# Routing attention and a PReLU feed-forward on one core: general-path test from the denominators, queries' clusters by DMA, members on ScalarE, fetch apart from split

## The chip, the cores and the metric

The kernel runs on one NeuronCore of a Trainium2 chip. The core has five engines with a queue of their own, each worked off in the order in which the program was written: TensorE (PE, matrix products; its weight loads are shown as PEld), VectorE (DVE), ScalarE (ACT), GpSimd (POOL) and SyncE (SP, which here only starts DMA transfers). They wait for each other by semaphores. SBUF is the working memory of 128 partitions, PSUM the eight banks that TensorE writes to. The metric is device time in microseconds (us) of one execution, as the median of several.

## The reference

Attention over 4 batches, 8 heads, 768 positions and a head size of 64, in which a query sees only the keys whose nearest of 16 centroids (by cosine) is its own, followed by a two-layer feed-forward with a PReLU:

```python
q_assign = np.argmax(np.einsum('bhsd,hcd->bhsc', q_n, c_n), axis=-1)
k_assign = np.argmax(np.einsum('bhsd,hcd->bhsc', k_n, c_n), axis=-1)
mask = q_assign[:, :, :, None] == k_assign[:, :, None, :]
scores = scale * np.matmul(q, k.transpose(0, 1, 3, 2))
scores = np.where(mask, scores, -1000000000.0)
attn = np.exp(scores - np.max(scores, axis=-1, keepdims=True))
attn = attn / (np.sum(attn, axis=-1, keepdims=True) + 1e-09)
attn_out = np.matmul(attn, v)
...
x = np.ascontiguousarray(attn_out.transpose(0, 2, 1, 3)).reshape(B * S, H * D)
h = x @ w_in
g = np.maximum(h, 0.0) + alpha * np.minimum(h, 0.0)
return g @ w_out
```

q, k, v and centroids are float32. The two weight matrices (512 x 2048 and 2048 x 512) and alpha arrive as the program's inputs; the weights are float64, and the kernel makes float32 of them itself out of their two 32-bit words.

## The kernel before, in words

**Pairs, units, steps.** Work goes by pairs n of two heads: n = 4 b + hp, 16 pairs. A unit is a pair and a half of its 384 queries, and it goes over the 6 chunks of 128 keys. The order of units is: batch, half, pair of heads, so four units make one block of 384 token rows over all 512 columns, and eight such blocks go to the feed-forward. A unit has three steps u, so there are 96 steps, NS. Steps 0 to 11 make the first block with attention alone; from step 12 on (UB) the feed-forward of the block before is woven in. Up to step 23 (TOGETHER is 24) a step treats two chunks; from step 24 on a unit treats its six chunks in two halves of three at its beginning, and the rest of its time is feed-forward, which the document calls the later stage.

**Slots.** A step has five slots: `tick()` at the beginning of each runs the pieces that `later(k, ...)` had put k slots ahead. In steps up to 23 the first two slots hold scores (`score`) and the weighing of what was scored the step before (`weigh`), the other three feed-forward pieces (`feed`) and preparations of later pairs (`prepare`). In the later stage a unit has three slots for its attention and twelve others, and a list `todo` of twelve entries is worked off, one in each, before the feed-forward piece of that slot: three masks, five additions into `acc`, the turn of `acc` with its row sums, an empty entry, `total`, `invert`. A block has 28 pieces: 16 `hidden` (four matrix products each and two evictions on ScalarE) and 12 `final` (four products each). `whole * left // 48` spreads them over the 48 slots of a block. After the last slot of a unit one more piece is fed where an accumulation is unfinished. When step 24 begins, two pieces have been kept back.

**Scores to output.** `score` multiplies keys by queries into a PSUM tile `sps` (two of them; the third chunk of a half uses two `fps` banks) and ScalarE takes Exp into one of the E tiles (L483, L486). For the pairs 0 to 3 (`n < NCH`) the cluster mask is a further product into the same bank (L475): `member` holds for each key a row of 0 or minus 2^60 per cluster, `aq` the queries' one-hot clusters. For later pairs VectorE masks (L499). `weigh` multiplies E by v into the single `vps` bank (L577), and for the first block also sums the denominators with a product by ones into `first_den` (L570). Otherwise denominators come from additions of E on VectorE (`add_up`, L510), a transposition and a row sum (`turn` L516, `rows_sums` L522, tile `part`), and a small product by `fold` (`total`, L532) into `mps`, the only bank of pool `ps_m`, which the products for similarities (`prep_sims`, L352) and clusters (`prep_clusters`, L397) use too. `invert` (L542 on) takes reciprocals and spreads them with two transpositions into `rd`; `normalise` (L606) multiplies `vps` by it into `xT`.

**Preparing a pair.** For pairs 0 to 3: `prep_features` transposes q and k on TensorE and ScalarE copies them out (L315, L319) in the step four ahead of the pair's first unit; three steps ahead of the pair's first unit `prep_sims` makes similarities, and one slot later `prep_argmax` finds each row's cluster on VectorE: transposition L360, maxima and comparisons L365 to L378, transposition to `member` (L382), and two scalings of its lower half by the columns of `pick` (L385). One step ahead of each of the pair's units `prep_queries` brings the queries' rows of `member` to the partitions 64 to 127 of `aq` (L425), two pieces of 32 rows. Later pairs return from `prep_argmax` before `member`; `prep_blocks` (VectorE), `prep_clusters`, `prep_keys` and transpositions (L429) take the place.

**Squares.** For every pair and each of q and k, `square` lets ScalarE square the raw tile four slots later, in place, with the sum of each row in `squares` (L327). At the end the greatest of these sums and the lowest denominator (`lowest`, L544, L587) make `good`; a product by ones makes a flag (L834) that decides whether a slow general path is run. With these inputs it is not.

**Weights.** 32 blocks of 128 x 512 numbers are converted one after the other in three stages: fetch and `split` (VectorE, L239, L241), four slots later `scale` (ScalarE, L245, L247), two slots later `join` (VectorE L251, L254; GpSimd L257). Five `raw` tiles are used in turn, so a fetch waits for the join of five conversions before. `converting` begins 15 of them in steps 0 to 11 and two in each step after that. `convert_up_to` would run a conversion at once if a feed-forward piece needed it.

**SyncE's queue** holds, in the program's order, the loads of q, k, v, the fetches of weights and the output rows.

Of the kernel before, what the change touches and what calls it, by code (L numbers as in the profile page):

```python
# [9 lines left out]
FP32 = mybir.dt.float32  # L10
BF16 = mybir.dt.bfloat16
U32 = mybir.dt.uint32
I32 = mybir.dt.int32
AF = mybir.ActivationFunctionType
ALU = mybir.AluOpType
AX = mybir.AxisListType
PS = bass.MemoryType.PSUM
P = 128
# [3 lines left out]
def kernel(  # L22
# [11 lines left out]
    nc = tc.nc  # L34
# [4 lines left out]
    NJ = S // P  # L39
# [4 lines left out]
    SCALE = float(D) ** -0.5  # L44
# [45 lines left out]
    def later(slots, piece):  # L90
        due.setdefault(now[0] + slots, []).append(piece)
# [8 lines left out]
    NP = len(pairs)  # L100
    raw_qk, vts = {}, {}

    Q = 32
# [127 lines left out]
    def convert(src, dst):  # L231
        raw = raw_tiles[0]
        raw_tiles.append(raw_tiles.pop(0))
        nc.sync.dma_start(out=raw.rearrange("p n w -> p (n w)"), in_=src)
        lo, hi = raw[:, :, 0], raw[:, :, 1]
        power = cvt.tile([P, CW], U32, name="power")

        def split():
            nc.vector.tensor_scalar(out=power, in0=hi, scalar1=0x7FF00000, scalar2=None,  # L239
                                    op0=ALU.bitwise_and)  # L240
            nc.vector.tensor_scalar(out=dst.bitcast(U32), in0=hi, scalar1=0x000FFFFF,  # L241
                                    scalar2=None, op0=ALU.bitwise_and)

        def scale():
            nc.scalar.activation(out=power, in_=power, func=AF.Relu,  # L245
                                 bias=low_exp[:, 0:1], scale=8.0)
            nc.scalar.activation(out=dst, in_=dst.bitcast(U32), func=AF.Identity,  # L247
                                 bias=1.0, scale=2.0 ** -20)

        def join():  # L250
            nc.vector.scalar_tensor_tensor(  # L251
                out=power, in0=hi, scalar=0x80000000, in1=power,
                op0=ALU.bitwise_and, op1=ALU.bitwise_or)
            nc.vector.scalar_tensor_tensor(  # L254
                out=dst, in0=lo, scalar=2.0 ** -52, in1=dst,
                op0=ALU.mult, op1=ALU.add)
            nc.gpsimd.tensor_tensor(out=dst, in0=dst, in1=power.bitcast(FP32),  # L257
                                    op=ALU.mult)
        return [split, scale, join]

# [34 lines left out]

    squares = const.tile([P, 2 * NP], FP32, name="squares")  # L300
    lowest = const.tile([P, 2 * NP], FP32, name="lowest")
    BOUND = 30.0 / SCALE


    qkTs, firsts, aqs = {}, {}, {}
# [3 lines left out]
    def prep_features(n, g):  # L309
        if n not in qkTs:  # L310
            qkTs[n] = qkp.tile([P, NB * P], FP32, name="qkT")
        ps = misc()
        for i, t in enumerate(groups[g]):
            w, j = divmod(t, NJ)
            nc.tensor.transpose(out=ps[:, i * P:(i + 1) * P],  # L315
                                in_=raw_qk[n, w][:, j].rearrange("p h d -> p (h d)"),
                                identity=ident)
        t0, m = groups[g][0], len(groups[g])
        later(1, lambda: nc.scalar.copy(qkTs[n][:, t0 * P:(t0 + m) * P],  # L319
                                        ps[:, 0:m * P]))  # L320
        for w in range(2):
            if t0 < (w + 1) * NJ <= t0 + m:
                square(n, w)

    def square(n, w):
        raw = raw_qk.pop((n, w)).rearrange("p j h d -> p (j h d)")
        later(4, lambda: nc.scalar.activation(  # L327
            out=raw, in_=raw, func=AF.Square,
            accum_out=squares[:, 2 * n + w:2 * n + w + 1]))

    def prep_blocks(n, w):
        if w == 0:
            qkTs[n] = qkp.tile([P, NB * P], FP32, name="qkT")
        nc.vector.transpose(out=qkTs[n][:, w * S:(w + 1) * S],
                            in_=raw_qk[n, w].rearrange("p j h d -> p (j h d)"))
        square(n, w)

# [18 lines left out]
    def prep_argmax(n, ps):  # L358
# [23 lines left out]
        nc.vector.transpose(out=member[:, 0, :], in_=top.rearrange("p t c -> p (t c)"))  # L382

        for h in (1, 0):
            nc.vector.tensor_scalar(  # L385
                out=member[HP:P, h, :], in0=member[HP:P, 0, :],
                scalar1=pick[HP:P, h:h + 1], scalar2=pick[HP:P, h + 2:h + 3],
                op0=ALU.mult, op1=ALU.add)
        members[n] = member

    def prep_clusters(n):
# [24 lines left out]
    def prep_queries(n, half, h):  # L416

        if h == 0:
            aqs[n, half] = aqp.tile([P, 2, HS], BF16, name="aq")
        if n < NCH:  # L420

            if h == 0:
                r = slice(half * Q, (half + 1) * Q)
                for g in range(NG // 2, NG):
                    nc.scalar.copy(aqs[n, half][g * Q:(g + 1) * Q, 0, :],  # L425
                                   members[n][r, 0, :])
            return
        own_half = everys[n].rearrange("p g i r h -> p g (i r) h")[:, half, :, h:h + 1]
        nc.vector.transpose(out=aqs[n, half][:, h, :],  # L429
                            in_=own_half.broadcast_to((P, NX, Q)))  # L430
# [105 lines left out]
    def invert(n, half):  # L536

        if (n, half) not in totals:
# [1 line left out]
        ps = totals.pop((n, half))  # L540
        inv = rdp.tile([P, 2 * NX], FP32, name="inv")
        nc.vector.reciprocal(out=inv, in_=ps[:, 0:2 * NX])  # L542
        i = 2 * n + half
        nc.vector.tensor_reduce(out=lowest[:, i:i + 1], in_=ps[:, 0:2 * NX], axis=AX.X,  # L544
                                op=ALU.min)
        rd = rdp.tile([P, HS], FP32, name="rd")
        for h in range(2):
            r = slice(h * D, (h + 1) * D)
# [5 lines left out]
    def weigh(m, denominators=False):  # L554
# [24 lines left out]
        if denominators and done:  # L579
# [3 lines left out]
            nc.vector.transpose(  # L583
                out=denT[:, 0:NX // 2, :].rearrange("p x i -> p (x i)"),
                in_=first_den[:, 0:HS // 2])
            i = 2 * n + half
            nc.vector.tensor_reduce(out=lowest[:, i:i + 1], in_=denT[:, 0:NX // 2, 0],  # L587
                                    axis=AX.X, op=ALU.min)
            inv = rdp.tile([P, 2 * NX], FP32, name="inv")
            for g in range(P // Q):  # L590
                h, x = divmod(g, 2)
# [131 lines left out]
    for u in range(-AHEAD, TOGETHER):  # L723
# [31 lines left out]
            feed_block(u)  # L755
            whole = len(ffn) - KEEP
        take = (max(len(ffn) - KEEP - whole * (UB - 1 - u % UB) // UB, 0) if ffn else 0)
        converting = 0 if u < 0 else 1 + (u % 4 == 3) if u < UB else 2
        for i in range(SLOTS - FIRST):
            tick()  # L760
            feed(take * (i + 1) // 3 - take * i // 3)
# [10 lines left out]
    for u in range(TOGETHER, NS + 1):  # L772
# [4 lines left out]
        if s == 0 or u == NS:  # L777
# [24 lines left out]
                todo.append(lambda c=c, E=E: add_up(E[c]))  # L802
            todo.append(lambda n=n, half=half: (turn(n, half), rows_sums(n, half)))
            todo.append(lambda: None)
            todo.append(lambda n=n, half=half: total(n, half))
            todo.append(lambda n=n, half=half: invert(n, half))
            slots = range(3, SLOTS)
        else:
            slots = range(SLOTS)
# [14 lines left out]
    while due:  # L824
        tick()
    good = const.tile([P, 2], FP32, name="good")
    nc.vector.tensor_reduce(out=good[:, 0:1], in_=squares, axis=AX.X, op=ALU.max)
    nc.vector.tensor_reduce(out=good[:, 1:2], in_=lowest, axis=AX.X, op=ALU.min)
    nc.vector.tensor_scalar(out=good[:, 0:1], in0=good[:, 0:1], scalar1=BOUND,
                            scalar2=None, op0=ALU.is_le)  # L830
    nc.vector.tensor_scalar(out=good[:, 1:2], in0=good[:, 1:2], scalar1=0.0,
                            scalar2=good[:, 0:1], op0=ALU.is_gt, op1=ALU.mult)
    flag = misc()
    nc.tensor.matmul(out=flag[0:1, 0:1], lhsT=good[:, 1:2], rhs=ones[:, 0:1],  # L834
                     start=True, stop=True)
# [160 lines left out]
```

## Time and profile before

| | |
|---|---|
| median of three runs | 1034.42 us (1032.88 to 1034.53) |
| profiled execution | 1034.78 us, its span 1032.9 us |
| TensorE busy | 1000.6 us, 97% |
| VectorE busy | 668.5 us, 65% |
| ScalarE busy | 353.9 us, 34% |
| GpSimd busy | 50.0 us, 5% |
| first scores / first feed-forward product | 17.27 us / 89.11 us after the span's start |

How to read it: a group or a timeline entry names the line of the kernel, the engine, the operation, and the tile written and the tiles read. An entry of the timeline begins with its start and its duration in us; "x8" are eight instructions in a row (a float32 matrix product counts as two); what stands in brackets is how long the engine stood idle before it, and whose work ended the wait. Where an instruction waited for more than one thing, the one that came last is named. The list of waits adds such idle times up: us in total, times, the longest. The span is divided into 40 slices of 25.8 us, with the busy share of each in tenths; PEclk is the clock granted to TensorE, in tenths of full speed. Ends of TensorE's products are modelled.

### The profile page before, as it was taken

To read this page: it belongs to the slowest core of one execution; us is meant where nothing else is said; L and a number is where in the kernel's file an instruction comes from. 1 tells how busy PE (TensorE), PEld (TensorE's weight loads), DVE (VectorE), ACT (ScalarE), POOL (GpSimd) and SP (SyncE) were. 2 spreads that over 40 slices of the span, in tenths; PEclk is the share of its full clock that TensorE was granted. 3 is DMA by queue.
4 is the path that set the end of the run, shared out by engine and by line. 5 is a ranking of instruction groups with operands and counts; after the bars stand their busy time and mean duration, and the time that the engine had idled before them with its cause. 6 is when DMAs were issued, how large, how long until landed. Compare 5 with 4: busy or idle time off the path is not lost.

```text
span 1032.9 us, 10431 instructions
## 1 busy us (share of the span) xinstructions
PE 1000.6 (97%) x3923; PEld 487.7 (47%) x3923; DVE 668.5 (65%) x1159; ACT 353.9 (34%) x692; POOL 50.0 (5%) x71
## 2 busy tenths in 40 slices
PE   7789999999999999999999999999999999999997
PEld 4334444454454544445454454545445454544453
DVE  4788798687475766778666666868756675662111
ACT  5756554434231323424132232414323141321220
POOL 1222322000000000000000000000000000000000
PEclk9989999999999999999999999999999999999999
DMA  9633654030000233040000230213000000000000
GB/s 194 184 112 104 149 132 87 16 77 0 1 1 20 41 47 46 1 87 5 1 0 11 52 47 10 36 36 56 1 1 1 31 0 1 1 11 20 1 0 34
DMA packets 120938, 42.74 MB, mean 41 GB/s; under 512 B 113696, under 2 KB 113712, under 8 KB 120880
## 3 DMA queue, kind: packets, MB, share of 16 engines
q1 hardware_dynamic: 120704, 41.95, 18.5%
q8 instruction: 33, 0.54, 0.2%
q14 instruction: 25, 0.20, 0.1%
q10 hardware_dynamic: 176, 0.04, 0.0%
HBM read 35.69 MB, written 6.29 MB: 41 GB/s over the span
## 4 chain that ended last, share of the span: by engine, by line
PE 87%; DVE 8%; ACT 3%; issue 1%; POOL 0%; DVEq 0%; POOLq 0%; ACTq 0%
PE fps L649 30%; PE fps L629 29%; PE vps L577 11%; PE sps L465 9%; PE fps L465 3%; DVE acc L510 2%; PE mps L352 1%; DVE acc L516 1%; PE sps L475 1%; PE mps L532 1%; DVE gT L621 1%; DVE part L522 1%; PE fps L570 1%; ACT gT L636 0%; DVE power L251 0%
## 5 line engine op out<-in xcount | busy, mean ns | idle before, releaser
L629 PE MATMUL fps<-xT,w_in_sb 128*128 128x384 f32 x1024 | 342.2, 491 | 0.0
L649 PE MATMUL fps<-w_out_sb,gT 128*128 128x512 f32 x768 | 337.1, 595 | 1.1 <-DVE gT L621 1.1
L629 PEld LDWEIGHTS fps<-xT,w_in_sb 128*128 128x128 f32 x1024 | 191.3, 190 | 141.9 <-ACT raw L483 4.9
L649 PEld LDWEIGHTS fps<-w_out_sb,gT 128*128 128x128 f32 x768 | 144.6, 190 | 176.2 <-issue 164.3
L621 DVE SCALAR_TENSOR_TENSOR gT<-neg,alpha_neg,gT 128x384 f32<-128x384 f32 x128 | 81.2, 637 | 125.9 <-ACT neg L637 124.4
L636 ACT ACTIVATE gT<-fps 128x384 f32<-128x384 f32 x128 | 62.7, 490 | 273.5 <-PE fps L629 273.5
L465 PE MATMUL sps<-qkT 64*128 64x384 f32 x576 | 113.1, 512 | 0.1
L499 DVE SCALAR_TENSOR_TENSOR raw<-aq,key,raw 128x384 f32<-128x384 bf16 x160 | 88.8, 614 | 37.7 <-ACT raw L486 26.2
L486 ACT ACTIVATE E<-sps 128x768 f32<-128x768 f32 x88 | 67.2, 814 | 65.5 <-PE sps L475 39.3
L499 DVE SCALAR_TENSOR_TENSOR E<-aq,key,E 128x384 f32<-128x384 bf16 x128 | 71.3, 613 | 17.9 <-ACT E L486 12.2
L577 PE MATMUL vps<-E,vt 128*64 128x384 f32 x448 | 82.9, 498 | 0.0
L465 PEld LDWEIGHTS sps<-qkT 64*128 64x128 f32 x576 | 53.1, 192 | 53.1 <-issue 22.1
L510 DVE TENSOR_TENSOR acc<-acc,E 128x768 f32<-128x768 f32 x64 | 61.2, 956 | 15.0 <-ACT E L486 13.2
L657 DVE TENSOR_TENSOR y<-y,fps 128x512 f32<-128x512 f32 x30 | 20.6, 686 | 69.1 <-PE fps L649 69.1
L637 ACT ACTIVATE neg<-fps 128x384 f32<-128x384 f32 x128 | 62.1, 485 | 0.0
L486 ACT ACTIVATE raw<-sps 128x768 f32<-128x768 f32 x56 | 42.9, 815 | 53.2 <-PE sps L465 53.2
L655 ACT COPY y<-fps 128x512 f32<-128x512 f32 x24 | 14.0, 585 | 133.3 <-PE fps L649 133.3
L577 PE MATMUL vps<-raw,vt 128*64 128x384 f32 x320 | 56.5, 491 | 0.0
L577 PEld LDWEIGHTS vps<-E,vt 128*64 128x64 f32 x448 | 29.4, 137 | 41.1 <-issue 41.1
L510 DVE TENSOR_TENSOR acc<-acc,raw 128x768 f32<-128x768 f32 x48 | 45.9, 956 | 1.1
L465 PE MATMUL fps<-qkT 64*128 64x384 f32 x192 | 41.5, 509 | 0.0
L483 ACT ACTIVATE raw<-fps 128x384 f32<-128x384 f32 x48 | 21.0, 495 | 48.1 <-PE fps L465 48.1
(101 smaller groups left out, 642.0 us busy)
## 6 DMA issues: line engine op xcount, KB each, us to landing
raw<-in_moe_w_in_dram SPq DMA_DIRECT2D x16, 512.0 KB, 4.0
raw<-in_moe_w_out_dram SPq DMA_DIRECT2D x16, 512.0 KB, 3.5
vt<-in_v_dram SPq DMA_DIRECT2D x16, 384.0 KB, 4.2
out_dram<-y SPq DMA_DIRECT2D x24, 256.0 KB, 2.1
qk<-in_q_dram SPq DMA_DIRECT2D x48, 96.0 KB, 4.0
qk<-in_k_dram SPq DMA_DIRECT2D x48, 96.0 KB, 3.5
qk<-in_q_dram SPq DMA_DIRECT2D x8, 192.0 KB, 4.1
qk<-in_k_dram SPq DMA_DIRECT2D x8, 192.0 KB, 4.3
```

The costliest lines, as they stand in the source:

```text
L465: nc.tensor.matmul(out=bank(ps, h), lhsT=qkT[r:r + D, S + c * P:S + (c + 1) * P], rhs=qkT[r:r + D, half * HS:(half + 1) * HS], start=True, ...
L483: nc.scalar.activation(out=E[:, h, :], in_=ps[h][:, 0:HS], func=AF.Exp, scale=SCALE)
L486: nc.scalar.activation(out=E, in_=ps[:, :, 0:HS], func=AF.Exp, scale=SCALE)
L499: nc.vector.scalar_tensor_tensor(out=E[:, h, :], in0=aqs[n, half][:, h, :], scalar=keys[n][:, NJ + c, h:h + 1], in1=E[:, h, :], op0=ALU.is ...
L510: nc.vector.tensor_tensor(out=acc, in0=acc if first is None else first[3], in1=E, op=ALU.add)
L577: nc.tensor.matmul(out=po[r:r + D, 0:HS], lhsT=vts[n][:, h, c, :], rhs=e[:, h, :], start=(c == 0), stop=(c == NJ - 1))
L621: nc.vector.scalar_tensor_tensor(out=gs[f], in0=neg, scalar=alpha_neg[:, f:f + 1], in1=gs[f], op0=ALU.mult, op1=ALU.add)
L629: nc.tensor.matmul(out=ps[:, 0:HS], lhsT=w_in_sb[:, c, f * P:(f + 1) * P], rhs=xT[:, c, :], start=(c == 0), stop=(c == NCH - 1))
L636: nc.scalar.activation(out=gs[f], in_=ps[:, 0:HS], func=AF.Relu)
L637: nc.scalar.activation(out=neg, in_=ps[:, 0:HS], func=AF.Relu, scale=-1.0)
L649: nc.tensor.matmul(out=ps[:, 0:DM], lhsT=gs[f][:, i * P:(i + 1) * P], rhs=w_out_sb[:, f, :], start=on and f == f0, stop=off and f == f0 + ...
L657: nc.vector.tensor_tensor(out=ys[i], in0=ys[i], in1=ps[:, 0:DM], op=ALU.add)
```

## The change

- `squares` and `square` are gone. The test for the general path uses the denominators alone: a second reduction keeps their highest value beside the lowest, both over the float32 words read as integers, and `good` compares them with the words of 2^-40 and 2^50.
- The scaling of the lower half of `member` (two per pair, pairs 0 to 3) is done by ScalarE instead of VectorE.
- The queries' rows go from `member` to `aq` by DMA on SyncE's queue instead of by ScalarE.
- A conversion of weights has four stages: fetch, two slots later split, four slots later scale, two slots later join. The first begins in step 1 instead of 0, and two are begun in every third step instead of every fourth; 15 are again begun by step 11.
- In the later stage `todo` has a second empty entry ahead of `total`, and no `invert`; `invert` is called in the next unit, behind the first half of its scores, by the call that stood there already and had found nothing to do.

```diff
@@ convert
-        nc.sync.dma_start(out=raw.rearrange("p n w -> p (n w)"), in_=src)
         lo, hi = raw[:, :, 0], raw[:, :, 1]
         power = cvt.tile([P, CW], U32, name="power")
+
+        def fetch():
+            nc.sync.dma_start(out=raw.rearrange("p n w -> p (n w)"), in_=src)
...
-        return [split, scale, join]
+        return [fetch, split, scale, join]
@@
-    squares = const.tile([P, 2 * NP], FP32, name="squares")
     lowest = const.tile([P, 2 * NP], FP32, name="lowest")
-    BOUND = 30.0 / SCALE
+    highest = const.tile([P, 2 * NP], FP32, name="highest")
+    WORDS = [float((127 + e) * 2 ** 23) for e in (-40, 50)]
+
+    def check(n, half, dens):
+        i = 2 * n + half
+        for to, op in ((lowest, ALU.min), (highest, ALU.max)):
+            nc.vector.tensor_reduce(out=to[:, i:i + 1], in_=dens.bitcast(I32), axis=AX.X,
+                                    op=op)
@@ prep_features, square, prep_blocks
-        for w in range(2):
-            if t0 < (w + 1) * NJ <= t0 + m:
-                square(n, w)
-
-    def square(n, w):
-        raw = raw_qk.pop((n, w)).rearrange("p j h d -> p (j h d)")
-        later(4, lambda: nc.scalar.activation(
-            out=raw, in_=raw, func=AF.Square,
-            accum_out=squares[:, 2 * n + w:2 * n + w + 1]))
...
-        square(n, w)
@@ prep_argmax
         for h in (1, 0):
-            nc.vector.tensor_scalar(
-                out=member[HP:P, h, :], in0=member[HP:P, 0, :],
-                scalar1=pick[HP:P, h:h + 1], scalar2=pick[HP:P, h + 2:h + 3],
-                op0=ALU.mult, op1=ALU.add)
+            nc.scalar.activation(
+                out=member[HP:P, h, :], in_=member[HP:P, 0, :], func=AF.Identity,
+                scale=pick[HP:P, h:h + 1], bias=pick[HP:P, h + 2:h + 3])
@@ prep_queries
                 for g in range(NG // 2, NG):
-                    nc.scalar.copy(aqs[n, half][g * Q:(g + 1) * Q, 0, :],
-                                   members[n][r, 0, :])
+                    nc.sync.dma_start(out=aqs[n, half][g * Q:(g + 1) * Q, 0, :],
+                                      in_=members[n][r, 0, :])
@@ invert
-        i = 2 * n + half
-        nc.vector.tensor_reduce(out=lowest[:, i:i + 1], in_=ps[:, 0:2 * NX], axis=AX.X,
-                                op=ALU.min)
+        check(n, half, ps[:, 0:2 * NX])
@@ weigh
-            i = 2 * n + half
-            nc.vector.tensor_reduce(out=lowest[:, i:i + 1], in_=denT[:, 0:NX // 2, 0],
-                                    axis=AX.X, op=ALU.min)
+            check(n, half, denT[:, 0:NX // 2, 0])
@@ steps up to 23
-        converting = 0 if u < 0 else 1 + (u % 4 == 3) if u < UB else 2
+        converting = 0 if u < 1 else 1 + (u % 3 == 2) if u < UB else 2
@@ later stage
             todo.append(lambda n=n, half=half: (turn(n, half), rows_sums(n, half)))
             todo.append(lambda: None)
+            todo.append(lambda: None)
             todo.append(lambda n=n, half=half: total(n, half))
-            todo.append(lambda n=n, half=half: invert(n, half))
@@ the end
-    nc.vector.tensor_reduce(out=good[:, 0:1], in_=squares, axis=AX.X, op=ALU.max)
+    nc.vector.tensor_reduce(out=good[:, 0:1], in_=highest, axis=AX.X, op=ALU.max)
     nc.vector.tensor_reduce(out=good[:, 1:2], in_=lowest, axis=AX.X, op=ALU.min)
-    nc.vector.tensor_scalar(out=good[:, 0:1], in0=good[:, 0:1], scalar1=BOUND,
+    nc.vector.tensor_scalar(out=good[:, 0:1], in0=good[:, 0:1], scalar1=WORDS[1],
                             scalar2=None, op0=ALU.is_le)
-    nc.vector.tensor_scalar(out=good[:, 1:2], in0=good[:, 1:2], scalar1=0.0,
-                            scalar2=good[:, 0:1], op0=ALU.is_gt, op1=ALU.mult)
+    nc.vector.tensor_scalar(out=good[:, 1:2], in0=good[:, 1:2], scalar1=WORDS[0],
+                            scalar2=good[:, 0:1], op0=ALU.is_ge, op1=ALU.mult)
```

## The prediction

> **What bounds the kernel now.** I read the page's engine shares and slices first. The columns are busy microseconds, share of the span and instruction count, or tenths in 40 slices of 25.8 us.
>
> ```profile
> PE 1000.6 (97%) x3923; PEld 487.7 (47%) x3923; DVE 668.5 (65%) x1159; ACT 353.9 (34%) x692; POOL 50.0 (5%) x71
> ...
> PE   7789999999999999999999999999999999999997
> ...
> PEclk9989999999999999999999999999999999999999
> ```
>
> TensorE is the bound: from about 90 us on it is busy nearly without a break, and only work taken from it, or its own idle time, can shorten the program there. Before 90 us it has holes. So the second view is the list of what TensorE waited for (total us, times, longest):
>
> ```profile
> PE fps L315 <- ACT qkT L319: 9.2, 4, 4.1
> PE mps L532 <- ACT every L401: 7.1, 10, 1.0
> PE sps L475 <- ACT aq L425: 2.9, 2, 2.7
> PE mps L532 <- DVE part L522: 2.0, 7, 0.3
> ```
>
> Two places matter. L532 is the little matmul of `total`: 17 waits, 9.1 us, all after 230 us. L315 and L475 are the start. Third, the timeline around one wait at L532:
>
> ```profile
> 418.14 0.25 PE L397 MATMUL mps<-first,spread 128*128 128x24 bf16 x4
> ...
> 419.10 0.25 ACT L401 CAST every<-mps 128x96 bf16<-128x96 f32 x1
> ...
> 419.40 0.40 PE L532 MATMUL mps<-part,fold 128*128 128x24 f32 x2 [1.01 <-ACT every L401]
> ...
> 419.64 2.83 PE L629 MATMUL fps<-xT,w_in_sb 128*128 128x384 f32 x8
> ...
> 422.40 1.56 PE L465 MATMUL sps<-qkT 64*128 64x384 f32 x8
> ```
>
> `prep_clusters` (L397) fills the only `mps` bank, ScalarE must copy it out, and `total` needs the bank: 1.0 us idle, with a feed-forward piece of 2.8 us waiting just behind. In the seven short cases it is the row sum `part` that ends late (0.2 to 0.3 us). Fourth, the timeline of the start, which shows how ScalarE's order of work makes TensorE's holes:
>
> ```profile
> 23.34 1.51 ACT L486 ACTIVATE E<-sps 128x768 f32<-128x768 f32 x2
> ...
> 24.51 0.58 DVE L382 STREAM_TRANSPOSE member<-top 128x384 bf16<-128x384 bf16 x1
> ...
> 25.13 0.80 DVE L385 TENSOR_SCALAR member<-member,pick 64x384 bf16<-64x384 bf16 x2
> ...
> 25.36 1.56 PE L465 MATMUL sps<-qkT 64*128 64x384 f32 x8
> ```
>
> ```profile
> 39.40 1.52 ACT L486 ACTIVATE E<-sps 128x768 f32<-128x768 f32 x2 [0.65 <-PE sps L475]
> ...
> 43.43 0.58 DVE L382 STREAM_TRANSPOSE member<-top 128x384 bf16<-128x384 bf16 x1
> ...
> 45.33 0.72 ACT L245 ACTIVATE power<-power,low_exp 128x512 uint32<-128x512 uint32 x1 [3.29 <-DVE power L239]
> ...
> 46.48 1.49 ACT L486 ACTIVATE E<-sps 128x768 f32<-128x768 f32 x2
> ...
> 49.13 1.03 ACT L425 COPY aq<-member 32x384 bf16<-32x384 bf16 x2
> ...
> 50.82 1.12 PE L315 MATMUL fps<-ident,qk 128*128 128x128 f32 x4 [4.11 <-ACT qkT L319]
> ```
>
> An Exp (L486) runs as soon as its scores exist, except where ScalarE stands at something older: at 45.33 it waited 3.29 us for a split (L239) that stood on VectorE behind the cluster search. TensorE paid with 4.11 us idle.
>
> **The change, part by part.** Each term is against the profiled execution: 1034.78 us (span 1032.9 and 1.88 around it), 0.36 above the median 1034.42.
>
> *Total one slot later.* In the later stage a unit has 12 slots (0 to 11) and a block's 28 pieces go to 48 slots: after slot i of unit k, floor(7(47-i)/12) - 7k are left, that is 22, 22, 21, 21 at slots 8 to 11. Slot 10 always feeds a piece, slots 9 and 11 none. `total` stood in slot 10 before that piece and now stands in slot 11, after it. The piece's 2.7 us (final pieces: 3.5) is more than any of the 17 waits (at most 1.0). The exception is the first block, 30 pieces because two were kept: its units 0 and 2 feed in slots 9 and 11, so the wait at 236.23 (1.0 us) stays. Term: 9.1 - 1.0 = -8.1 us. `invert` moves behind the next unit's scores; on VectorE nothing lies between the two places. At 422.63 its reciprocal ran after the scores had begun anyway, so it costs nothing; the cover is 1.6 us until the first Exp is out, and VectorE's other 35% idle.
>
> *No squares.* 32 activations of 0.862 and 32 accumulator reads of 0.218: 34.6 us less on ScalarE, which is 34% busy. TensorE has no wait for a square in its list; zero. They also held the raw tiles: SyncE's queue waited 6.5 us on them in two places, and the loads behind were early enough; zero.
>
> *Second reduction.* 32 of 0.12 (24 columns) to 0.16 us (6 columns), 4 us of VectorE in its idle third. Zero; at the start four of 0.16 at most.
>
> *Queries' clusters by DMA.* 16 copies of 0.508 leave ScalarE, 16 DMAs of 24 KB enter SyncE's queue. No row shows an on-chip copy. Nearest by size: 8 and 32 KB landed in 3.0 and 2.3 us; behind a load it would be a load's 3.5 to 4.3. I take 4.3, as the first follows load(2). Ready at 14.5 (end of L382), needed at 19.75 by L475: 5.2 us, it fits by 0.9; the others have eight or more. Ends: 0 and +2 for the first alone. Behind each waiting copy stand the weights' fetches: the first starts near 14.7 either way, and those after the copy for pair 1 start at 25.1 or later and are split near 31 to 33. What is gained: ScalarE's 1.03 us ahead of L319 and the 2.9 us waits of L475.
>
> *Member on ScalarE.* L385 (0.383 on VectorE) becomes an activation; nearest rows: 0.490 for 128x384 (L636) and 0.508 (L425), so 1.0 a pair. The price is not this but the wait: ScalarE now stands at L382 with the next Exps queued behind, and the next scores wait for the Exps' banks. Worked for each pair:
> - Pair 0: ScalarE waited for the same L382 before (4.2 us, at the copies). Zero.
> - Pair 1: L382 ends 25.09, members 26.1, first Exp 26.9 instead of near 24.2; the next scores start at 27.0, not 25.36: +1.6.
> - Pair 2: the similarity matmuls end at 37.38, normalise at 38.17, the chain L360 to L382 takes 3.95 (10.55 to 14.50): 42.1. Members 43.1, one scaling (0.72 + 0.63) 44.5, then the Exps that ran at 39.40; first out at 45.3, TensorE was ready at 41.5: gap 3.8. After the 4.11 gap the granted clock fell, and against the same rows at full clock L315 took 1.12 for 0.66, L465 2.93 for 1.56, L475 0.82 for 0.50, L570 1.51 for 0.86: +2.8. So +6.6.
> - Pair 3: the same, +6.6.
>
> [...]
>
> *What is returned at the start.* Splits now run well ahead of their scaling (four slots, no longer behind the argmax), so the hold at 45.33 goes, and the copies at 49.13 with it: 4.11 + 2.8 = 6.9. The gap at 71.67 (2.66 + 0.22, then L577 2.35 for 1.51 and L465 2.37 for 1.56, 1.65) goes with the copies: 4.5. The copies at 30.11 sat in a gap of 1.20; half returns, 0.6. Together 12.0. Net: 14.8 - 12.0 = +2.8. Ends: +14.8 if nothing returns, -12.0 if the new waits are all covered. I stay near the middle since both sides come from the same in-order queue.
>
> *Conversions.* Fetch to join is 8 slots instead of 6, the first starts a step later; by step 12 both have begun 15, both begin the last in step 20. The last weights are joined by the start of step 22 and used in step 23; a raw tile has five slots between being free and being split, as before. Zero. VectorE's 9.5 us of waiting for the first fetches goes; behind it stood work that waited for L352 anyway.
>
> Sum: -8.1 + 2.8 = -5.3, so 1029.5 for a profiled execution, 1029.1 for the median.
>
> **Rivals.**
> - *ScalarE's new wait decides (slower).* Place: the Exps behind members of pairs 1 to 3. For it: strict order at 45.33. Against: the old holds should go. It decides as soon as the start loses over 8.1; at its full price +14.8 the net is +6.7: 1041.1.
> - *The start gains too.* VectorE is freed early, the members come before the Exps are ready. For: VectorE spent 9.5 us on DMA waits. Against: L352's time sets the chain. -8.1 - 12.0: 1014.3.
> - *The wait of total only moves.* If the bank or the row sum is late even after the piece, the change doesn't do what it seems to: 1034.4 + 2.8 = 1037.2. Against: 2.7 us of cover for 1.0.
> - *The copies land late.* First scores +2, each later one covered: 1031.
>
> **How the numbers follow.** Forecast 0.52, first rival 0.18, second 0.16, third 0.09, fourth 0.05. The forecast's own range is 1023 to 1034. The wider one runs from most of the second rival's way (1017) to just short of the first's full price (1040). Faster by over 0.2% (2.1 us, about what this measurement can tell from nothing) takes the forecast, the second and most of the fourth: 0.71. Slower takes the first and most of the third: 0.23; 0.06 between.
>
> **What will show it.** Right: no TensorE wait at L532 but one of 1.0 us in the first shared block; no wait of L475 for `aq`; gaps of about 3.8 us at the second-next scores after the similarity matmuls of pairs 2 and 3, with Exps behind the member activations; first feed-forward matmul near 92 instead of 89.1. Wrong: gaps at L532 as before, or the first feed-forward matmul after 97.

## The result: no difference, because two stages lost what the third gained

The changed kernel took 1033.88 us (median of four runs, 1032.59 to 1035.93), the kernel before 1033.86 beside it: a ratio of 1.0003, with a 95% interval of 0.9982 to 1.0024. The forecast was 1029.1. The profiled execution took 1034.77 us with a span of 1032.8, against 1034.78 and 1032.9 before, so the two profiles can be set side by side without a correction. The page of the changed kernel, its shares and slices:

```profile
PE 998.5 (97%) x3923; PEld 490.1 (47%) x3923; DVE 673.8 (65%) x1183; ACT 325.0 (31%) x620; POOL 52.5 (5%) x71
...
PE   7789999899999999999999999999999999999997
...
PEclk8899999999999999999999999999999999999999
```

Little of the change can be read there but ScalarE's busy time, 28.9 us less. The sum hides three stages that moved in different ways. I cut both traces at four instructions of TensorE: the first feed-forward product, the first scores of step 24, and the product for the general-path flag (L834 before, L828 after):

| stage | before | after | difference | forecast |
|---|---|---|---|---|
| start, to the first feed-forward product | 89.1 us | 92.8 us | +3.7 | +2.8 |
| middle, to step 24 | 119.5 | 128.5 | +9.0 | 0 |
| later stage, to the flag | 735.9 | 722.8 | -13.1 | -8.1 |
| end | 88.4 | 88.6 | +0.2 | 0 |

The list of TensorE's waits in the changed kernel answers the one shown of before (engine, line, whom it waited for: us in total, times, longest):

```profile
PE sps L463 <- ACT E L484: 10.3, 3, 4.0
PE fps L324 <- ACT qkT L328: 4.4, 3, 3.9
...
PE mps L351 <- DVE highest L310: 4.1, 2, 3.0
PE fps L623 <- DVE xT L600: 2.1, 1, 2.1
...
PE mps L530 <- DVE part L520: 1.3, 2, 0.7
...
PE mps L530 <- ACT every L399: 1.0, 1, 1.0
```

L530 is `total`, L532 before. Of its 17 waits of the later stage one is left, the 1.0 us in the first shared block; the two for `part` are new and lie in the middle (153 and 188 us). The waits of L475 for `aq` are gone, and three for Exps have come. L351 (`prep_sims`) and L623 (`hidden`) wait for VectorE, both in the middle. All line numbers from here on are those of the kernel that is spoken of.

The later stage, in the timeline of the changed kernel around the `total` that before stood at 419.40 with 1.01 us of waiting:

```profile
429.15 0.25 PE L395 MATMUL mps<-first,spread 128*128 128x24 bf16 x4
...
429.25 2.83 PE L623 MATMUL fps<-xT,w_in_sb 128*128 128x384 f32 x8
...
430.10 0.25 ACT L399 CAST every<-mps 128x96 bf16<-128x96 f32 x1
...
431.91 0.30 PE L530 MATMUL mps<-part,fold 128*128 128x24 f32 x2
...
432.14 1.56 PE L463 MATMUL sps<-qkT 64*128 64x384 f32 x8
```

The piece of 2.8 us lies where the gap was, ScalarE's copy is out 1.6 us before it is needed, and the scores follow `total` at once.

The start, in the timeline of the changed kernel:

```profile
45.85 0.58 DVE L381 STREAM_TRANSPOSE member<-top 128x384 bf16<-128x384 bf16 x1
...
46.47 1.43 ACT L384 ACTIVATE member<-member,pick 64x384 bf16<-64x384 bf16 x2 [5.03 <-DVE member L381]
...
47.92 0.72 ACT L247 ACTIVATE power<-power,low_exp 128x512 uint32<-128x512 uint32 x1
...
49.06 1.49 ACT L484 ACTIVATE E<-sps 128x768 f32<-128x768 f32 x2
49.91 2.93 PE L463 MATMUL sps<-qkT 64*128 64x384 f32 x8 [4.03 <-ACT E L484]
```

ScalarE stands idle for 5 us at the members, then does one scaling that had been due meanwhile, then the Exps; TensorE loses 4.03 us and runs the next scores in 2.93 instead of 1.56 us.

The middle, where the forecast had nothing, around the second wait of L351:

```profile
191.84 0.70 DVE L253 SCALAR_TENSOR_TENSOR power<-raw,power 128x512 uint32<-128x512 uint32 x1
...
192.44 0.70 DVE L256 SCALAR_TENSOR_TENSOR w_out_sb<-raw,w_out_sb 128x512 f32<-128x512 uint32 x1
193.05 0.70 DVE L253 SCALAR_TENSOR_TENSOR power<-raw,power 128x512 uint32<-128x512 uint32 x1
...
193.65 0.70 DVE L256 SCALAR_TENSOR_TENSOR w_out_sb<-raw,w_out_sb 128x512 f32<-128x512 uint32 x1
194.25 0.32 DVE L540 RECIPROCAL inv<-mps 128x24 f32<-128x24 f32 x1
194.47 0.14 DVE L310 TENSOR_REDUCE lowest<-mps 128x1 f32<-128x24 int32 x1
194.50 0.18 DVE L310 TENSOR_REDUCE highest<-mps 128x1 f32<-128x24 int32 x1
...
194.75 0.85 PE L351 MATMUL mps<-qkT,cT 128*32 128x384 f32 x8 [2.99 <-DVE highest L310]
```

The joins of two conversions (L253, L256) stand on VectorE directly ahead of the inversion, and the similarity products wait for the bank that the inversion reads. The same place before, where the wait was 0.44 us:

```profile
179.38 0.65 DVE L251 SCALAR_TENSOR_TENSOR power<-raw,power 128x512 uint32<-128x512 uint32 x1
...
179.95 0.68 DVE L254 SCALAR_TENSOR_TENSOR w_out_sb<-raw,w_out_sb 128x512 f32<-128x512 uint32 x1
...
181.60 0.30 DVE L542 RECIPROCAL inv<-mps 128x24 f32<-128x24 f32 x1
...
181.99 0.85 PE L352 MATMUL mps<-qkT,cT 128*32 128x384 f32 x8 [0.44 <-DVE lowest L544]
```

One join there, and the conversions' other stages are already done while TensorE is at its 7.1 us of output products. In the middle TensorE's waits grew from 1.5 to 8.3 us, and all of them are for VectorE. The gap of 2.07 us before L623 at 97.09 was followed by slow products: the granted clock was 0.58 from 97 to 100 us. The same 18 products, first in the changed kernel and then in "inversion first", an experiment below:

```profile
97.09 7.74 PE L623 MATMUL fps<-xT,w_in_sb 128*128 128x384 f32 x18 [2.07 <-DVE xT L600]
```

```profile
97.99 6.04 PE L623 MATMUL fps<-xT,w_in_sb 128*128 128x384 f32 x18 [1.94 <-DVE xT L600]
```

That is 1.7 us more. With the 6.8 us of waits it makes 8.5 of the 9.0.

### The profile page after: what moved, and what is told of

It is laid out like the page before. It is cut to its first block, busy times and chain, and to the rows that moved or that the text cites. A ratio compares the mean times of both kernels' runs of the same rounds, so it can differ in the third digit from the quotient of the medians.

```text
span 1032.8 us, 10335 instructions
## 1 busy us (share of the span) xinstructions
PE 998.5 (97%) x3923; PEld 490.1 (47%) x3923; DVE 673.8 (65%) x1183; ACT 325.0 (31%) x620; POOL 52.5 (5%) x71
## 4 chain that ended last, share of the span: by engine, by line
PE 87%; DVE 8%; ACT 2%; issue 1%; POOL 1%; DVEq 0%; POOLq 0%
PE fps L623 31%; PE fps L643 30%; PE vps L573 11%; PE sps L463 9%; PE fps L463 3%; PE mps L351 1%; DVE power L253 1%; DVE acc L508 1%; PE sps L473 1%; DVE w_out_sb L243 1%; ACT member L384 1%; DVE w_in_sb L256 1%; DVE power L241 0%; PE fps L324 0%; DVE w_out_sb L256 0%
## 5 line engine op out<-in xcount | busy, mean ns | idle before, releaser
L623 PE MATMUL fps<-xT,w_in_sb 128*128 128x384 f32 x1024 | 342.6, 492 | 2.1 <-DVE xT L600 2.1
L623 PEld LDWEIGHTS fps<-xT,w_in_sb 128*128 128x128 f32 x1024 | 192.1, 191 | 146.7 <-issue 7.8
L615 DVE SCALAR_TENSOR_TENSOR gT<-neg,alpha_neg,gT 128x384 f32<-128x384 f32 x128 | 78.3, 613 | 132.7 <-ACT neg L631 131.3
L463 PE MATMUL sps<-qkT 64*128 64x384 f32 x576 | 115.2, 520 | 10.3 <-ACT E L484 10.3
L497 DVE SCALAR_TENSOR_TENSOR E<-aq,key,E 128x384 f32<-128x384 bf16 x128 | 71.3, 613 | 11.9 <-ACT E L484 6.2
L508 DVE TENSOR_TENSOR acc<-acc,E 128x768 f32<-128x768 f32 x64 | 66.4, 1038 | 8.3 <-ACT E L484 6.5
```

Of the source, the lines that this page charges most:

```text
L463: nc.tensor.matmul(out=bank(ps, h), lhsT=qkT[r:r + D, S + c * P:S + (c + 1) * P], rhs=qkT[r:r + D, half * HS:(half + 1) * HS], start=True, ...
L497: nc.vector.scalar_tensor_tensor(out=E[:, h, :], in0=aqs[n, half][:, h, :], scalar=keys[n][:, NJ + c, h:h + 1], in1=E[:, h, :], op0=ALU.is ...
L508: nc.vector.tensor_tensor(out=acc, in0=acc if first is None else first[3], in1=E, op=ALU.add)
L615: nc.vector.scalar_tensor_tensor(out=gs[f], in0=neg, scalar=alpha_neg[:, f:f + 1], in1=gs[f], op0=ALU.mult, op1=ALU.add)
L623: nc.tensor.matmul(out=ps[:, 0:HS], lhsT=w_in_sb[:, c, f * P:(f + 1) * P], rhs=xT[:, c, :], start=(c == 0), stop=(c == NCH - 1))
```

## The experiments

Theory A: the middle's 9 us come from the conversions, whose stages stand later in the order of work on the engines. Rivals: they come from the start, whose delay is carried on (B); or a fetch apart from its split costs by itself. The table has all runs, with the stages from each profile (us), the median and the ratio to the kernel before on the same chip.

| kernel | start | middle | later | median | ratio, 95% interval |
|---|---|---|---|---|---|
| before | 89.1 | 119.5 | 735.9 | 1034 | |
| after | 92.8 | 128.5 | 722.8 | 1033.88 | 1.0003 (0.9982 to 1.0024) |
| after, old conversions | 94.0 | 119.7 | 722.8 | 1027.66 | 0.9940 (0.9924 to 0.9957) |
| after, members on VectorE | 91.0 | 128.6 | 722.8 | 1031.40 | 0.9969 (0.9956 to 0.9981) |
| before, later total alone | 87.6 | 119.5 | 722.8 | 1020.83 | 0.9873 (0.9857 to 0.9889) |
| after, neither | 87.7 | 119.7 | 722.8 | 1021.87 | 0.9883 (0.9866 to 0.9899) |
| after, five slots to the split | 101.5 | 129.3 | 722.8 | 1042.70 | 1.0075 (1.0057 to 1.0093) |
| before, new conversions alone | 91.8 | 128.7 | 735.9 | 1046.29 | 1.0107 (1.0088 to 1.0126) |
| after, neither, copies on ScalarE | 89.1 | 119.6 | 722.8 | 1022.06 | 0.9880 (0.9863 to 0.9898) |
| after, inversion first | 93.8 | 125.3 | 722.8 | 1031.38 | 0.9969 (0.9956 to 0.9982) |
| after, fetch two ahead | 94.0 | 119.7 | 722.8 | 1027.41 | 0.9942 (0.9924 to 0.9960) |
| after, fetch and split late | 90.2 | 128.6 | 722.8 | 1033.32 | 0.9998 (0.9989 to 1.0008) |
| the best parts | 83.0 | 120.6 | 722.8 | 1016.67 | 0.9843 (0.9818 to 0.9869) |

Middle and later stage repeat to 0.2 us between kernels of the same order; the start does not: "before" and "later total alone" run the same instructions there in the same order and took 89.1 and 87.6. So a difference of 1.5 us at the start means nothing. "After" and "fetch and split late" differ there by more than 2.5 us, with the same order on TensorE, VectorE, ScalarE and GpSimd.

**Old conversions.**

```diff
-        return [fetch, split, scale, join]
+        return [split, scale, join]
-        converting = 0 if u < 1 else 1 + (u % 3 == 2) if u < UB else 2
+        converting = 0 if u < 0 else 1 + (u % 4 == 3) if u < UB else 2
```

> The changed kernel with the conversions as before (fetch and split together, first in step 0). Between the first feed-forward product and step 24 the changed kernel took 128.5 us, the one before 119.5. Theory A: a conversion of four stages puts splits and joins into the first two slots of a step, on VectorE ahead of the inversion that the similarity products and the next normalisation wait for; that is the 9.0 us. It expects this stretch at 119 to 121 us, the start near the changed kernel's 92.8 (91 to 95), the later stage at its 722.8, and in all about 1025 us (1023 to 1028). Theory B: the stretch is long because the members on ScalarE make VectorE enter it late; then it stays at 126 us or more, and the whole at 1031 or more.

Middle 119.7 us, start 94.0, whole 1027.66. TensorE's waits in the middle of this kernel are those of before again:

```profile
PE fps L641 <- DVE gT L613: 1.1, 2, 0.9
...
PE mps L349 <- DVE highest L308: 0.5, 1, 0.5
```

The start is as long as in the changed kernel, and the middle is short all the same: rival B falls.

**Members on VectorE.**

```diff
-            nc.scalar.activation(
-                out=member[HP:P, h, :], in_=member[HP:P, 0, :], func=AF.Identity,
-                scale=pick[HP:P, h:h + 1], bias=pick[HP:P, h + 2:h + 3])
+            nc.vector.tensor_scalar(
+                out=member[HP:P, h, :], in0=member[HP:P, 0, :],
+                scalar1=pick[HP:P, h:h + 1], scalar2=pick[HP:P, h + 2:h + 3],
+                op0=ALU.mult, op1=ALU.add)
```

> The changed kernel with the members' scaling back on VectorE. The waits of TensorE for Exps behind the members (2.2, 4.0 and 4.0 us, and some 2.8 us of slow clock after each of the two long ones) should go: the first feed-forward product at 79 to 84 us instead of 92.8. Theory A: the stretch up to step 24 stays near 128 (126 to 131), in all about 1024 (1020 to 1028). Theory B: the stretch falls to about 120 as well, in all about 1013 to 1016.

The middle stayed at 128.6, as A says. The start did not fall to 79 to 84: the waits for Exps behind members are gone (0.6 us left), but others took their place. The first products for scores ran at 13.0 instead of 17.7 us, and their mask then waited 4.9 us for the first copy by DMA; further on TensorE lost 2.8 and 1.1 us to VectorE and 3.5 us to ScalarE's copies of features. My expectation had counted a wait as gone time without asking what is late next.

**Later total alone**, in the kernel before:

```diff
             todo.append(lambda: None)
+            todo.append(lambda: None)
             todo.append(lambda n=n, half=half: total(n, half))
-            todo.append(lambda n=n, half=half: invert(n, half))
```

> The kernel before with the later total and without the early inversion alone. From the profiles of the two kernels, units with a wait at the total lost 0.6 to 1.3 us in the changed kernel: step 24 to the flag 722.8 instead of 735.9. If that is this part's work: start 89.1 and middle 119.5 as before, later stage 722 to 724, in all 1020.5 to 1022.5. If instead the later stage gained from the squares' absence, the whole stays above 1027.

1020.83 us, with the later stage at 722.8 to the tenth. The whole gain of the change is in these two lines; the squares have no part in it. Which of the two it is, the later `total` or the inversion taken from behind it, no run separates.

**Neither** conversions nor members:

> The changed kernel with both undone: old conversions, members on VectorE; what is left of the change is no squares, the copies by DMA, the second reduction and the later total. If the two undone parts are all that was lost, the start is at most the 89.1 of before, less what the missing copies and squares gave TensorE (the 1.2 us gap, the 2.9 us waits): 82 to 89; the middle 119 to 121, the later stage 722 to 724, in all 1014 to 1022. If the copies by DMA cost something too, the start is above 89 and the whole above 1022.

1021.87 us, start 87.7. Its first scores wait in the same place as above. The timeline of this kernel:

```profile
13.92 0.58 DVE L379 STREAM_TRANSPOSE member<-top 128x384 bf16<-128x384 bf16 x1
...
14.67 2.32 SPq L422 DMA_DIRECT2D aq<-member  x2
...
19.35 0.98 PE L472 MATMUL sps<-aq,member 32*128 32x384 bf16 x4 [4.87 <-DMA aq<-member]
```

Issued at 14.67, there at 19.3. But the start as a whole is no longer than before, so others that went pay for this wait: the 4.11 us of before at 50.82 are 2.99 here, and the 1.20 at 31.80 and the 2.66 at 71.67 are gone, while 1.1 and 2.7 us of waiting for VectorE are new. From "neither", the new conversions add 9.5 us (to "members on VectorE"), the members on ScalarE 5.8 (to "old conversions"), and both 12.0: they overlap in part.

**Five slots to the split.** A first attempt to keep the fetch apart and move the stages out of the first two slots of a step:

```diff
-            later(4 if len(stages) == 2 else 2, lambda: stages and advance(stages))
+            later({3: 5, 2: 3, 1: 2}[len(stages)], lambda: stages and advance(stages))
```

> The changed kernel with five slots from fetch to split, then three to the scaling and two to the join: ten slots in flight instead of eight, but splits and joins now fall in the slots 2 to 4 of a step, where feed-forward pieces are fed, and none in its first two. Theory A (the place of the stages costs the middle its 9 us) expects the stretch from the first feed-forward product to step 24 at 119 to 122 us instead of 128.5, and in all 1024 to 1028. Rival (a fetch apart costs by the time in flight, by raw tiles coming free later): the stretch stays at 128 or grows, and the whole is 1034 or more.

Theory A, in the form that the first two slots of a step are the wrong place, falls here: no split and no join stands in them (the scalings on ScalarE do), and the middle is 129.3. The waits are partly others:

```profile
PE fps L643 <- DVE gT L615: 3.7, 2, 2.9
...
PE mps L351 <- DVE highest L310: 2.5, 1, 2.5
...
PE fps L623 <- DVE xT L600: 1.0, 1, 1.0
```

The slopes of the feed-forward now stand behind joins. The start grew to 101.5 with two gaps of 7.7 us before scores whose Exps stood late on ScalarE. The rival was right in its numbers; but this kernel changes both the time in flight and the order on the engines, so it could not say which.

**New conversions alone**, in the kernel before (the edit of the old conversions, turned round):

> The kernel before with the four-stage conversions alone. Theory A: the middle grows from 119.5 to 127 to 130 us with nothing else of the change there, the start stays at 87 to 93, the later stage at 735.9: 1041 to 1046 in all. If the middle's loss needs the other parts (members or copies elsewhere, the second reduction), it is below 1038.

1046.29 us: start +2.7, middle +9.2, later stage as before. The conversions need nothing else of the change to cost 12 us. This run also tests what the prediction expected of them at the start, that splits run ahead of their scaling and the 4.11 us gap at 50.82 goes:

```profile
44.12 0.72 ACT L247 ACTIVATE power<-power,low_exp 128x512 uint32<-128x512 uint32 x1 [2.72 <-DVE power L241]
...
46.79 1.03 ACT L427 COPY aq<-member 32x384 bf16<-32x384 bf16 x2
...
51.30 1.12 PE L317 MATMUL fps<-ident,qk 128*128 128x128 f32 x4 [4.46 <-ACT qkT L321]
52.34 2.93 PE L467 MATMUL sps<-qkT 64*128 64x384 f32 x8
```

ScalarE still waits 2.72 us for the split, the copies still stand behind it, and TensorE still loses 4.46 us and runs the next scores in 2.93 us instead of 1.56.

**Copies on ScalarE**, with conversions and members as before too:

> What is left of the change when conversions, members and the queries' copies are all as before: the later total, no squares, the second reduction. In the kernel with the copies by DMA the first scores waited 4.9 us for the first copy (issued at 14.67, landed at 19.3); by ScalarE it would be there at about 15.6. If that wait is on the path, the start is 84 to 86 us instead of 87.7 and the whole 1018 to 1020; if the start is set by VectorE anyway, it is 87 to 89 and the whole 1020 to 1023, as with the later total alone.

1022.06 us, start 89.1: as "neither" and as "later total alone", within their intervals. Taken together, the copies by DMA, the second reduction and the missing squares are worth nothing that these runs can tell, in either direction.

**Inversion first**, in the changed kernel:

```diff
+        if ended:
+            invert(*prior[:2])
         tick()
         if u >= 0:
             score(n, half, range(s, NJ, SB))
         tick()
-        if ended:
-            invert(*prior[:2])
```

> The changed kernel, with the inversion in steps up to 23 called ahead of the first slot of the next step instead of after its second: on VectorE it now stands before the split and the joins that fall into those two slots. Theory A expects the waits of the similarity products for the denominators' reductions (1.1 and 3.0 us) to go and the middle to fall from 128.5 to 122 to 126 us, the whole to 1027 to 1031; the wait of the first feed-forward products (2.1 us) and those at the total (0.6 and 0.7) stay. If the order ahead of the inversion is not the cause, the middle stays at 128 or more.

The waits of L351 fell from 4.1 to 0.6 us and the middle to 125.3; the whole, 1031.38, is just above what was expected. So the joins ahead of the inversion are the cause of L351's waits. The 3.2 us that the middle lost are not all theirs: the waits for `part` grew to 1.6, and one of 1.5 came at a `hidden` product, for an output addition on VectorE, so TensorE's waits fell by 1.8 us in all, from 8.3 to 6.5. The rest is mostly the 18 products at 97.99: they took 6.04 us here instead of 7.74, which is the pace of before (24 of them in 8.01 us from 89.11), although the gap before them, which the edit leaves alone, was still 1.94 us.

**Fetch two ahead.** The pair that separates the fetch from the order. Here each fetch is issued two conversions ahead of its split, while VectorE, ScalarE and TensorE have the order of "old conversions", instruction by instruction:

```diff
     def convert_next():
-        if sources:
-            under_way.append(convert(*sources.popleft()))
-            advance(under_way[-1])
+        if not fetched:
+            fetch_next()
+        if fetched:
+            under_way.append(fetched.popleft())
+            advance(under_way[-1])
+        while sources and len(fetched) < 2:
+            fetch_next()
...
-        converting = 0 if u < 1 else 1 + (u % 3 == 2) if u < UB else 2
+        converting = 0 if u < 0 else 1 + (u % 4 == 3) if u < UB else 2
...
+        if u == -1:
+            fetch_next()
+            fetch_next()
```

> The changed kernel with a fetch apart from its split, but another way: each fetch is issued two conversions ahead, and split, scaling and join stand in the slots they had before the change. On VectorE, ScalarE and TensorE the instructions are in the same order as in the kernel with the old conversions (middle 119.7, whole 1027.7); only SyncE's fetches stand earlier. Theory A, in the form that is left (it is where split, scaling and join stand on VectorE and ScalarE, two slots later): the middle is 119 to 121 us, the whole 1024 to 1029. Rival (a fetch apart from its split costs, for whatever reason): the middle is 126 or more, the whole 1034 or more.

Middle 119.7, whole 1027.41: the same as "old conversions" in every stage.

**Fetch and split late.** The reverse, with the order of the changed kernel on the three engines:

```diff
         def fetch():
-            nc.sync.dma_start(out=raw.rearrange("p n w -> p (n w)"), in_=src)
+            pass

         def split():
+            nc.sync.dma_start(out=raw.rearrange("p n w -> p (n w)"), in_=src)
```

> The reverse: the changed kernel, in which each fetch is issued only where its split stands, two slots late, so that fetch and split are together again; the order on VectorE, ScalarE and TensorE is that of the changed kernel. Theory A: the middle stays at 127 to 130 us and the whole at 1033 to 1038. Rival: the middle returns to 119 to 122 and the whole to 1024 to 1029.

Middle 128.6, whole 1033.32. The fetch's place has no effect, and the order of split, scaling and join has all of it. What VectorE itself waits for in the middle differs between the two orders. Before, and then after:

```profile
DVE power L239 <- POOL w_in_sb L257: 3.9, 3, 1.4
...
DVE power L239 <- POOL w_out_sb L257: 2.3, 2, 1.2
```

```profile
DVE power L241 <- POOL w_in_sb L259: 5.5, 4, 1.4
DVE power L241 <- POOL w_out_sb L259: 5.5, 4, 1.4
```

17 splits and 19 joins are begun in the middle in both. In the changed kernel eight splits wait 1.4 us each, all of them directly behind a join; before, five waited 1.2 to 1.4 us. Each starts 0.03 us after the end of the GpSimd product of the conversion three before it, and the pool that `power` comes from, `cvt`, has three buffers (`bufs=3`): what the split waits for is its buffer. That is 4.8 us more of waiting on VectorE, in order, ahead of all that stands behind. Besides, VectorE's busy time in the middle grew from 95.7 to 100.7 us. No run gave `power` a fourth buffer or took this waiting away by itself, so how much of the middle is due to it stays open.

**The best parts**: the later total, no squares, members on VectorE, the copies by DMA except the two for the very first scores, fetches two ahead.

```diff
+                    if (n, half) == (0, 0):
+                        nc.scalar.copy(aqs[n, half][g * Q:(g + 1) * Q, 0, :],
+                                       members[n][r, 0, :])
+                        continue
                     nc.sync.dma_start(out=aqs[n, half][g * Q:(g + 1) * Q, 0, :],
                                       in_=members[n][r, 0, :])
```

> A version from the parts that cost nothing: the later total, no squares, members' scaling on VectorE, the conversions' stages where they were with fetches two ahead, the copies by DMA except those for the very first scores, which ScalarE makes (their DMA kept TensorE waiting 4.9 us). If these waits of the start are on the path: start 82 to 86 us instead of 87.6 to 89.1, middle 119 to 121, later stage 722.8, in all 1015 to 1020. If the start is set by VectorE's own work: 87 to 89 and 1020 to 1023, no better than the later total alone.

1016.67 us, 0.9843 of the kernel before (0.9818 to 0.9869), and the shortest median of all kernels here. The start is 83.0. The waits for members, for the first copy and for `aq` are gone; the two longest of those that stay at the start are:

```profile
PE fps L337 <- ACT qkT L341: 7.2, 3, 3.9
...
PE vps L591 <- DVE xT L618: 2.7, 1, 2.7
```

So the parts of the change seem to help at the start where none of them opens a wait of its own: 83.0 is 4.6 us below "later total alone". The evidence is not strong. The intervals of these two kernels overlap, one of the four runs here took 1020.39 us, and "neither" differs in two things, the first copies and the fetches, which no run separates.

## Why the prediction was wrong

- *Conversions.* This is the step that failed: "Fetch to join is 8 slots instead of 6 ... a raw tile has five slots between being free and being split, as before. Zero." All that it checks holds: no weight came late, and a fetch's place is worth nothing (fetch two ahead). It asked when the weights are needed and when `raw` is free, and not which work stands behind the moved stages, nor when a buffer of `power` is free. On VectorE that work is the row sums, the inversion and the first block's last normalisation; the cost was +9.0 us in the middle, and 11.9 for the conversions alone. VectorE's idle third, which the prediction counts on for the second reduction and the inversion, is an average over the program; in the middle VectorE was busy for 95.7 of 119.5 us already before.
- *Total one slot later.* The mechanism was right to the piece: 16 of 17 waits went, the one in the first shared block stayed. The term was mis-sized: -8.1 was the idle time alone, and the stage gave -13.1. A unit with a wait of 1.01 us (28.92 us long) became 1.27 shorter, one with 0.31 became 0.67. The rest beside the idle time is 0.26 to 0.36 us in all but one of the 16 units that lost a wait (0.17 there), and up to 0.09 in units that had none. L532's weight load waited too (1.10 us idle at 419.40), and its two small products took 0.40 us together there, against 0.30 at the same place in the changed kernel (431.91), where nothing waited. That is 0.10 us of it; what the rest is was not shown.
- *Member on ScalarE.* Right: gaps of 2.2, 4.0 and 4.0 us for the 1.6, 3.8 and 3.8 worked out, with the scores after the long ones at 2.93 us as in the row that I had used. The activation took 0.70 us, not 0.5. That the gap of pair 1 would be followed by slow rows too (2.82 us for the scores instead of 1.56, at a granted clock of 0.54) I had not counted.
- *What is returned at the start.* The gaps at 31.80, 50.82 and 71.67 are gone and the start came out at +3.7 for +2.8, within what it varies by, but for the largest of these terms this was luck. The prediction gave 6.9 us to splits that run ahead. They do not: with the new conversions alone the gap stayed, at 4.46 us, and "old conversions" lacks it as the changed kernel does. In both, TensorE now idles in front of the scores instead (4.88 and 4.03 us). The copies by DMA shorten the gap: 2.99 us in "neither", 3.52 with the new conversions added. Of VectorE's 9.5 us of waiting for the first fetches, 5.0 stayed.
- *Queries' clusters by DMA.* Right in size: 4.6 us for the 4.3 taken. In the changed kernel ScalarE's members hid it, as the first scores come only at 17.7 us there; it showed where they were moved back.
- *No squares, second reduction.* Zero, as said.
- *The clock.* The granted clock was 0.54 in the 3 us after a gap of 2.2 us, 0.58 in the 3 us after one of 2.07, and 1.00 after one of 2.99. In these rows of the changed kernel a stretch and its length are followed by the busy time and instructions of PE, PEld, DVE, ACT and POOL, then by the granted clock; the last two columns are the DMA's share and GB/s:

```profile
29.00:32.00 3.00, 2.94 (x10) 1.20 (x12) 0.00 (x0) 0.71 (x2) 0.00 (x0) 0.54 0.81 277
97.00:100.00 3.00, 2.91 (x5) 1.63 (x6) 1.55 (x3) 1.65 (x4) 0.00 (x0) 0.58 0.00 0
194.75:197.75 3.00, 3.00 (x13) 1.21 (x14) 2.88 (x5) 0.00 (x0) 1.97 (x2) 1.00 0.01 1
```

The gap at 97.09 cost 1.7 us beside its own 2.07 (7.74 against 6.04 us for the 18 products). For each of the two gaps of 4 us the prediction had taken 2.8 us of slow rows, those behind the 4.11 us gap of before. That was too much: the scores took 2.93 us behind both, as there, but the mask's products 0.65 and 0.50 us for the 0.82 taken, the products by ones 0.86 for 1.51, and no products for features, 0.46 of the 2.8, stood behind these gaps. The slow rows cost 1.5 and 1.4 us.

Of the rivals none happened. The result lies inside the range of the forecast's own case, 1023 to 1034, for a reason that was in none.

## What to carry to other kernels

When a stage of work is moved by some slots, read on every engine what stands directly behind its new place and who waits for that; that its own result is still in time says nothing about it. Look at every buffer that the moved work uses, not only at the largest. An engine's idle share of the whole program is no cover in a stage in which it is fuller. That a sum of terms comes out right does not show that its terms are. And a change of several parts that measures as nothing is worth taking apart: here two lines gained 1.3%, and two other parts gave it back.

## What the runs showed of the hardware that was not expected

- TensorE's granted clock was 0.54 and 0.58 in the 3 us after gaps of 2.2 and 2.07 us in the changed kernel (29.07 and 97.09); after one of 1.20 us, before (31.80), it was 1.00. Between 2 and 3 us a gap's length alone does not decide: after 2.99 us in the changed kernel (194.75) it was 1.00, and after 1.94 in "inversion first" (97.99) the products ran at the pace of before. What else decides is not shown here.
- A copy of 24 KB from SBUF to SBUF by DMA took 4.6 us behind loads in "neither", and 3.3, 3.8 and 3.7 as the median of 16 in the changed kernel, "neither" and "members on VectorE", where ScalarE's copy takes 0.51.
- A removed wait of TensorE in the later stage gave back mostly 0.26 to 0.36 us more than its idle time.
